# Chunked attention and a feed-forward layer on one core: v's maximum in two halves, an alternating place for weight-block sums, and later hi and lo parts

## Chip, cores and metric

The kernel runs on one core of one Trainium2 chip. The metric is the device time of one execution in microseconds; the median of several runs is compared. Before the change the median of 3 runs is 870.75 us (869.64 to 871.2).

## The reference

Attention inside chunks of 64 positions, then `h = x @ w_in`, `g = h - tanh(h)`, `g @ w_out`, all in float32:

```python
q_c = q.reshape(B, H, nc, chunk, D)          # 8, 8, 9, 64, 64; k and v alike
scores = scale * np.matmul(q_c, k_c.transpose(0, 1, 2, 4, 3))
scores = scores - np.max(scores, axis=-1, keepdims=True)
attn = np.exp(scores)
attn = attn / (np.sum(attn, axis=-1, keepdims=True) + 1e-09)
out = np.matmul(attn, v_c)
...
x = out.transpose(0, 2, 1, 3).reshape(B * S, H * D)     # 4608 x 512
h = x @ w_in                                            # 512 x 2048
g = h - np.tanh(h)
return (g @ w_out).astype(np.float32)                   # 2048 x 512
```

## The kernel before

The 4608 tokens are worked on in nine groups of 512, numbered 0 to 8. Attention fills a group's x; the feed-forward layer then takes the group in units. float32 accuracy is kept by splitting operands into a hi and a lo part (float16 in the later stages) and adding three products.

Groups 0, 1 and 2 go through `FeedForward` (16 units each, one for each block of 128 rows of the hidden layer). Groups 3 to 8 go through `Fast`: 16 units to a group, unit (b, j) taking half the group's tokens (b) and the weight-block pair (j, j + 8). In a unit PE runs `gemm1` (24 matmuls into one of two PSUM tiles `ph`), ACT the tanh (L644), DVE the difference (L645), POOL three sums for a seven-product scheme of the second matrix product (L646 to L648), and one unit later ACT and DVE make hi and lo of it (L657, L658). `gemm2` of a unit follows three units after its `gemm1`; at a new half of the tokens one unit has none and the next has two. `finish` (L688 and its neighbours) turns the PSUM sums of a half into output rows.

While a group is in the feed-forward layer, the next group's attention is prepared between its units. The function `ahead` names the place: `put(unit, part, f)`, where part 0 lies ahead of the unit's gemm2 and part 1 behind it. First comes a common scale: ACT sums |q| and |k| (L107, units 1 and 2), DVE takes the largest |v| (L125, L126, unit 4), PE transposes these `sums` (`across`, L293, unit 4 part 1), DVE takes their maximum over partitions (`most`, L295), and PE spreads it (`spread_out`, L302, unit 5). DVE makes powers of two of it (L119 to L121, L507 to L512). Units 6 and on split q, k and v (L322, L323), multiply scores (L333, unit 8), and so on for the two halves of the group. The raw tensors are loaded two 128-token pairs at a time, in units 7 and 15 of the group before.

The seven-product scheme needs sums of the second weights. For each pair j `Half.combine` adds on POOL: the first sum w1 (L474) into the first free place, then the second (L477) and three more steps (L480 to L485). `Half.shorten` makes hi and lo of the four results on ACT (L502) and DVE (L503). Pairs 0 to 5 are done in group 2's stage; pairs 6 and 7 run over into the first units of `Fast`, placed by a list of positions at the end of the kernel.

Inside these stages the schedule is manual: every engine keeps the order in which the code is written. An engine works its queue strictly in that order, so one instruction that waits holds all behind it.

The step whose place in the queues the prediction speaks of:

```python
largest(some.rearrange("p i n -> p (i n)"), d["sums"][:, 2:3])
```

Of the kernel before, what the change touches and what calls it, by code (L numbers as in the profile page):

```python
# [11 lines left out]
F32 = mybir.dt.float32  # L12
# [6 lines left out]
ALU = mybir.AluOpType  # L19
AX = mybir.AxisListType  # L20
PSUM = bass.MemoryType.PSUM

P = 128
# [16 lines left out]
FAST = 3  # L40
# [19 lines left out]
def attn_ffn_kernel(ctx: ExitStack, tc: tile.TileContext, qE, kE, vE, qL, kL, vL, w_in, w_out, out):  # L60
# [8 lines left out]
    nc = tc.nc  # L69
# [19 lines left out]
    def place_of(a, part, fc, dtype=F16):  # L89

        return w_pool[fc].tile([P, DM], F32R, name=f"w{a}{part}{fc}").bitcast(dtype)
# [8 lines left out]
    def new_half_x():  # L100

        t = xpool.tile([P, KC, MOST], F32R, name="xh").bitcast(F16)
        return t[:, :, :MOST], t[:, :, MOST:]
# [149 lines left out]
    class Late:  # L253
# [14 lines left out]
        def sums(self, g, n, other=None):  # L268
# [13 lines left out]
            if other is None:  # L282
                self.scales(g)

        def scales(self, g):
            self.across(g)
            self.spread_out(g)
# [135 lines left out]
    class Half:  # L423
# [42 lines left out]
        def combine(self, j):  # L466

            (h1, l1), (h2, l2) = ([t.bitcast(F32) for t in wt[fc][1]] for fc in (j, j + FC // 2))  # L470
            names = [(a, 1, fc) for fc in (j, j + FC // 2) for a in "hl"]
            free = self.free
            w1 = place_of(*free[0], F32)
            nc.gpsimd.tensor_add(w1, h1, l1)  # L474
            yield
            w2 = place_of(*names[0], F32)
            nc.gpsimd.tensor_add(w2, h2, l2)  # L477
            yield
            x, y = (place_of(*n, F32) for n in names[1:3])
            nc.gpsimd.tensor_sub(x, w2, w1)  # L480
            yield
            nc.gpsimd.tensor_add(y[:, :HD], w1[:, :HD], w1[:, HD:])
            nc.gpsimd.tensor_add(y[:, HD:], w2[:, :HD], w2[:, HD:])
            yield
            nc.gpsimd.tensor_add(w1[:, HD:], w1[:, :HD], w2[:, HD:])  # L485
            self.sums[j] = w1, x, y, w2[:, HD:]
            parts = [place_of(*n).rearrange("p (a n) -> p a n", a=2) for n in (names[3], free[1], free[2])]
            if j % 2 == 0:
                self.last = place_of(*free[3])
            parts.append(self.last[:, (j % 2) * DM:(j % 2 + 1) * DM].rearrange("p (a n) -> p a n", a=2))  # L490
            self.dest[j] = parts
            self.free = [free[0], *names[:3], *free[3 + (j % 2 == 0):]]
            a, b, c, d = parts
            left, right = slice(0, HD), slice(HD, DM)
            fast_w[j] = {1: a[:, :, right], 2: a[:, :, left], 3: b[:, :, right], 4: b[:, :, left], 5: d, 6: c[:, :, left], 7: c[:, :, right]}
            yield
# [19 lines left out]
    class FeedForward:  # L516
# [54 lines left out]
        def run(self, units, at, ahead=None):  # L571
            for s in range(len(units) + LAG):
                if ahead:
                    ahead(s)
                if s < len(units):
                    self.gemm1(*units[s])
                    self.shrink()
                    self.split()
                for f in at.pop(2 * s, []):
                    f()  # L580
                if len(self.queue) > min(LAG, len(units) + LAG - 1 - s):
                    self.gemm2()
                for f in at.pop(2 * s + 1, []):
                    f()
            assert not at, at
            self.finish()
# [152 lines left out]
    def ahead(att, at, g):  # L739

        o = 2 * FC * (g - FAST)

        def put(unit, part, f, *args):
            at[o + 2 * unit + part].append(lambda: f(*args))

        for unit, n in (1, "q"), (2, "k"), (4, "v"):
            put(unit, 0, lambda n=n: att.sums(g, n, ffn.tile([P, MOST], F32, name="t", bufs=3)))
        put(4, 1, att.across, g)
        put(5, 0, att.spread_out, g)
        put(5, 1, lambda: powers.update({g: half.power_of(g)}))  # L750
        put(6, 0, lambda: xs.update({g: new_half_x()}))
        for b, u in enumerate((6, 14)):
            put(u, 0, att.split, g, b, "q")
            put(u + 1, 0, att.split, g, b, "k")
            put(u + 1, 1, att.split, g, b, "v")
            if g + 1 < NG:
                for i in (2 * b, 2 * b + 1):
                    put(u + 1, 1, att.load, FIRST[g + 1] + i, i)
            put(u + 2, 0, att.scores, g, b)
            put(u + 2, 1, att.shifted, g, b)  # L760
            put(u + 3, 0, att.exponent, g, b)
            put(u + 3, 1, att.totals, g, b)
            put(u + 4, 0, att.divided, g, b)
            put(u + 5, 0, att.transpose, g, b)
            at[o + 2 * u + 16].insert(0, lambda b=b: att.values(g, b, xs[g]))
# [15 lines left out]
    att = Early(pool, [psum, ps_a], 4, warm)  # L781
# [70 lines left out]
    att, half = Late(late), Half(late)  # L852
# [26 lines left out]
    for g in range(FAST, NG):  # L879
        ahead(att, at, g)  # L880
    made = {}

    def make(j, steps):
        if j not in made:
            made[j] = half.combine(j)
        for _ in range(steps):
            next(made[j])
# [5 lines left out]
    o = 2 * FC  # L893
    for k, j, steps in (o - 1, 6, 2), (o + 1, 6, 2), (o + 3, 6, 1), (o + 4, 7, 1), (o + 5, 7, 1), (o + 6, 7, 1), (o + 7, 7, 1), (o + 8, 7, 1):
        at[k].append(lambda j=j, steps=steps: make(j, steps))
    for k, j, some in (o + 6, 6, slice(0, 2)), (o + 8, 6, slice(2, 4)), (o + 11, 7, slice(0, 2)), (o + 15, 7, slice(2, 4)):
        at[k].append(lambda j=j, some=some: half.shorten(j, some))
    at[o + 17].append(lambda: post.extend(place_of(*n, F32) for n in half.free[:3]))
    with tc.manual_schedule():
# [53 lines left out]
```

## Time and profile before

| | us |
|---|---|
| median of 3 runs | 870.75 |
| the profiled execution | 869.55 |
| its span, first to last instruction | 867.8 |
| PE busy | 826.6 |
| DVE busy | 655.5 |
| ACT busy | 469.8 |
| POOL busy | 354.0 |

Rows of instructions read: start, duration, engine, line, operation, output<-inputs, shapes, count, and in brackets the idle time of the engine just ahead with what ended it. A row of the view of waits reads: who waited <- for whom: total us, times, longest. A row of the chain of work that ended last reads: start, duration, what; "issue" is time in which nothing that the profile shows was waited for. A row of a stretch reads: from:to, length, then busy time of PE, PEld (weight loads), DVE, ACT and POOL, the granted clock as a share of full speed, and the DMA share and GB/s. Line numbers are those of the kernel before.

### The profile page before, as it was taken

What the parts mean: (1) busy time and instruction counts of PE and PEld (TensorE: products, weight loads), DVE (VectorE), ACT (ScalarE), POOL (GpSimd) and SP (SyncE); (2) the same over time, 40 slices, a digit from 0 to 9 for tenths busy, and PEclk for the clock granted to TensorE, in tenths of its full rate; (3) what the DMA queues carried; (4) which work ended last, traced back from release to release, by engine and by line L of the source; (5) the groups of instructions that cost most, each with busy time, mean ns of one, the idle gap of its engine ahead of it and who ended that gap; (6) DMA issues with size and microseconds to landing.
All of it is one profiled execution on the core that took longest, in us unless ns stands there. A gap on an engine that the chain in (4) does not pass through costs nothing.

```text
span 867.8 us, 20051 instructions
## 1 busy us (share of the span) xinstructions
PE 826.6 (95%) x8546; PEld 687.9 (79%) x8546; DVE 655.5 (76%) x885; ACT 469.8 (54%) x767; POOL 354.0 (41%) x368
## 2 busy tenths in 40 slices
PE   8999999999999998699979997999799979999996
PEld 6888777788756667588868886888688868888886
DVE  6897896778449988697858786878688777877563
ACT  7698786665345566354725463546444544444332
POOL 0000000000026667555635654565456554756563
PEclk8999999999999999799989999999999999999999
DMA  9973435220202123022212221222122210112000
GB/s 221 260 224 121 147 106 185 74 74 26 74 1 73 26 59 89 2 74 50 75 49 75 51 74 49 75 50 75 50 71 53 75 49 3 39 13 50 2 26 25
DMA packets 61401, 63.16 MB, mean 73 GB/s; under 512 B 32640, under 2 KB 40832, under 8 KB 61312
## 3 DMA queue, kind: packets, MB, share of 16 engines
q1 hardware_dynamic: 61312, 61.88, 25.3%
q8 instruction: 67, 1.10, 0.5%
q14 instruction: 22, 0.18, 0.1%
HBM read 45.09 MB, written 9.44 MB: 63 GB/s over the span
## 4 chain that ended last, share of the span: by engine, by line
PE 83%; DVE 8%; POOL 3%; ACT 3%; issue 3%; DMA 1%; SPq 0%; ACTq 0%; DVEq 0%; POOLq 0%
PE ph L637 27%; PE po L675 22%; PE po L569 14%; PE ph L540 13%; PE psa L333 3%; DVE sums L125 2%; PE psa L243 1%; PE psa L195 1%; DVE wh L688 1%; POOL xl L646 1%; POOL xl L647 1%; DVE gl L658 1%; DVE w L143 1%; ACT wh L657 1%; ACT gh L657 1%
## 5 line engine op out<-in xcount | busy, mean ns | idle before, releaser
L637 PE MATMUL ph<-xh,wl 128*128 128x256 f16 x2160 | 258.8, 279 | 0.0
L637 PEld LDWEIGHTS <-wl 128*128 128x128 f16 x2160 | 215.6, 100 | 29.7 <-issue 0.5
L644 ACT ACTIVATE t<-ph,sig 128x512 f32<-128x512 f32 x96 | 66.0, 687 | 214.7 <-PE ph L637 214.4
L646 POOL TENSOR_TENSOR xl<-xl 128x256 f32<-128x256 f32 x96 | 88.6, 923 | 225.4 <-DVE xl L645 225.4
L645 DVE SCALAR_TENSOR_TENSOR xl<-ph,sig,t 128x512 f32<-128x512 f32 x96 | 71.6, 746 | 82.1 <-ACT t L644 81.6
L675 PEld LDWEIGHTS <-wh 128*128 128x128 f16 x1008 | 97.3, 98 | 11.6
L647 POOL TENSOR_TENSOR xl<-xl 128x128 f32<-128x128 f32 x96 | 104.4, 1087 | 0.0
L675 PE MATMUL po<-wl,wh 128*128 128x256 f16 x576 | 91.7, 273 | 0.0
L648 POOL TENSOR_TENSOR xl<-xl 128x256 f32<-128x256 f32 x96 | 90.1, 939 | 0.0
L658 DVE SCALAR_TENSOR_TENSOR wh<-xl,to_g,wh 128x896 f16<-128x896 f32 x48 | 67.5, 1406 | 25.3 <-ACT wh L657 24.3
L658 DVE SCALAR_TENSOR_TENSOR gl<-xl,to_g,gh 128x896 f16<-128x896 f32 x48 | 75.0, 1563 | 8.4 <-ACT gh L657 8.4
L569 PE MATMUL po<-wh,gh 128*128 128x512 f32 x192 | 78.9, 411 | 0.7 <-ACT gh L559 0.7
L675 PE MATMUL po<-wh,wh 128*128 128x256 f16 x432 | 78.7, 273 | 0.0
L540 PE MATMUL ph<-xh,wl 128*128 128x512 f16 (+2 forms) x324 | 77.0, 375 | 0.0
L569 PE MATMUL po<-wl,gh 128*128 128x512 f32 x192 | 75.5, 393 | 0.0
L569 PE MATMUL po<-wh,gl 128*128 128x512 f32 x192 | 75.2, 396 | 0.0
L657 ACT ACTIVATE wh<-xl,to_g 128x896 f16<-128x896 f32 x48 | 49.7, 1035 | 44.0 <-POOL xl L648 44.0
L675 PEld LDWEIGHTS <-gh 128*128 128x128 f16 x672 | 64.9, 98 | 7.8
L474 POOL TENSOR_TENSOR wh<-wh,wl 128x512 f32<-128x512 f32 x8 | 14.2, 1779 | 107.2 <-DVE wl L463 75.6
L560 DVE TENSOR_TENSOR gl<-t,gh 128x512 fp32r<-128x512 f32 (+1 forms) x52 | 40.7, 785 | 20.3 <-ACT gh L559 18.1
L675 PE MATMUL po<-wh,gh 128*128 128x256 f16 x336 | 54.4, 273 | 0.0
L448 POOL PARTITION_ALL_REDUCE whole<-sums x1 | 0.4, 447 | 130.7 <-DMA rawv<-vL 130.7
(154 smaller groups left out, 1516.9 us busy)
## 6 DMA issues: line engine op xcount, KB each, us to landing
raw<-w_in SPq DMA_DIRECT2D x16, 512.0 KB, 4.0
raw<-w_out SPq DMA_DIRECT2D x16, 512.0 KB, 5.6
out<-wh SPq DMA_DIRECT2D x32, 256.0 KB, 2.2
rawk<-kL SPq DMA_DIRECT2D x28, 256.0 KB, 3.1
rawv<-vL SPq DMA_DIRECT2D x28, 256.0 KB, 3.6
xl<-qL SPq DMA_DIRECT2D x28, 256.0 KB, 3.1
qbd<-qE SPq DMA_DIRECT2D x16, 128.0 KB, 4.3
k<-kE SPq DMA_DIRECT2D x8, 256.0 KB, 4.4
```

What stands on the lines that cost most here:

```text
L540: nc.tensor.matmul(ph, lhsT=self.weight(fc, 0, a)[:, kc * P:(kc + 1) * P], rhs=x[b][:, kc, cols], start=(k == 0), stop=(k == 3 * KC - 1))
L560: nc.vector.tensor_sub(gl, t, gh)
L569: nc.tensor.matmul(self.po[t], lhsT=gg[a][:, ts], rhs=self.weight(fc, 1, b), start=(fc == 0 and i == 0), stop=(fc == FC - 1 and i == 2))
L637: nc.tensor.matmul(self.ph[:, 1 - f::2, :], lhsT=half_w[fc][:, w, kc * P:(kc + 1) * P], rhs=rhs, start=(k == 0), stop=(k == 3 * KC - 1))
L644: nc.scalar.activation(t, self.ph, AF.Tanh, scale=sig)
L645: nc.vector.scalar_tensor_tensor(out=u[:, :4], in0=self.ph, scalar=sig, in1=t, op0=ALU.mult, op1=ALU.subtract)
L646: nc.gpsimd.tensor_add(u[:, 4:6], u[:, 1:3], u[:, 0:4:3])
L647: nc.gpsimd.tensor_add(u[:, 6], u[:, 1], u[:, 2])
L648: nc.gpsimd.tensor_sub(u[:, 0:4:3], u[:, 0:2], u[:, 2:4])
L657: nc.scalar.activation(gh, u, AF.Copy, scale=powers[1])
L658: nc.vector.scalar_tensor_tensor(out=gl, in0=u, scalar=powers[1], in1=gh, op0=ALU.mult, op1=ALU.subtract)
L675: nc.tensor.matmul(place[m], lhsT=part[:, self.SUM[m]], rhs=w[m][:, o], start=first, stop=(j == FC // 2 - 1 and part is gl), skip_group_ch ...
```

## The change

Three edits.

1. A new function `halves` takes the largest |v| over two pairs (1024 elements of each partition) at a time, and joins the two results with the scaling in one small instruction. For groups 4 to 8 the first half stands three units ahead of the group's own first unit (unit 13 of the group before), for group 3 in unit 1; the second half stands in unit 2, part 1. Before, one maximum over 2048 elements stood in unit 4. The scale's other steps keep their places.
2. `combine`: with more than four free places, the first and the last change places before each pair, so that w1 of successive pairs goes to two places in turn.
3. `shorten` of pairs 6 and 7 is placed in later units: (o + 6, 8, 11, 15) becomes (o + 9, 11, 13, 15), counted in half units.

```diff
+        def halves(self, g, i):
+
+            d = self.st[f"g{g}"]
+            if i == 0:
+                d["v"] = self.pool.tile([P, 2], F32, name="v", bufs=2)
+            v = d["v"]
+            nc.vector.tensor_reduce(out=v[:, i:i + 1], in_=self.raw["v"][:, 2 * i:2 * i + 2].rearrange("p i n -> p (i n)"), axis=AX.X, op=ALU.max, apply_absolute_value=True)
+            if i:
+                nc.vector.tensor_scalar(out=d["sums"][:, 2:3], in0=v[:, 0:1], scalar1=v[:, 1:2], scalar2=2.0 ** -12, op0=ALU.max, op1=ALU.mult)
...
             free = self.free
+            if len(free) > 4:
+                free[0], free[-1] = free[-1], free[0]
             w1 = place_of(*free[0], F32)
...
-        for unit, n in (1, "q"), (2, "k"), (4, "v"):
+        for unit, n in (1, "q"), (2, "k"):
             put(unit, 0, lambda n=n: att.sums(g, n, ffn.tile([P, MOST], F32, name="t", bufs=3)))
+        put(-3 if g > FAST else 1, 0, att.halves, g, 0)
+        put(2, 1, att.halves, g, 1)
         put(4, 1, att.across, g)
...
-    for k, j, some in (o + 6, 6, slice(0, 2)), (o + 8, 6, slice(2, 4)), (o + 11, 7, slice(0, 2)), (o + 15, 7, slice(2, 4)):
+    for k, j, some in (o + 9, 6, slice(0, 2)), (o + 11, 6, slice(2, 4)), (o + 13, 7, slice(0, 2)), (o + 15, 7, slice(2, 4)):
         at[k].append(lambda j=j, some=some: half.shorten(j, some))
```

The new lines shift the numbers: L295 becomes L305, L302 becomes L312, L323 L333, L380 L390, L474 L486, L477 L489, L503 L515, L645 L657, L658 L670, L688 L700. L291 is the new maximum, L293 the instruction that joins the halves.

DVE's queue in units 2 to 5 of the period that prepares group 5, before, from the last row of `finish` (L688) on:

```order
L688 SCALAR_TENSOR_TENSOR wh_2610<-po_4610,minus_g,wl_4407 128x256
L645 SCALAR_TENSOR_TENSOR xl<-ph,sig,t 128x512
L658 SCALAR_TENSOR_TENSOR wh_2612<-xl,to_g,wh_2611 128x896
L380 TENSOR_TENSOR a<-s,a 128x2x512
L645 SCALAR_TENSOR_TENSOR xl<-ph,sig,t 128x512
L658 SCALAR_TENSOR_TENSOR wh_2614<-xl,to_g,wh_2613 128x896
L125 TENSOR_REDUCE sums<-rawv 128x1
L126 TENSOR_SCALAR sums<-sums 128x1
L295 TENSOR_REDUCE most<-psa 3x1
```

The same place on DVE now:

```order
L700 SCALAR_TENSOR_TENSOR wh_2610<-po_4612,minus_g,wl_4409 128x256
L291 TENSOR_REDUCE v<-rawv 128x1
L293 TENSOR_SCALAR sums<-v 128x1
L657 SCALAR_TENSOR_TENSOR xl<-ph,sig,t 128x512
L670 SCALAR_TENSOR_TENSOR wh_2612<-xl,to_g,wh_2611 128x896
L390 TENSOR_TENSOR a<-s,a 128x2x512
L657 SCALAR_TENSOR_TENSOR xl<-ph,sig,t 128x512
L670 SCALAR_TENSOR_TENSOR wh_2614<-xl,to_g,wh_2613 128x896
L305 TENSOR_REDUCE most<-psa 3x1
```

The end of the maximum has moved ahead of two units' work; `most` keeps its place behind it. The first half stands on DVE near the end of the period before:

```order
L670 SCALAR_TENSOR_TENSOR wh_2614<-xl,to_g,wh_2613 128x896
L657 SCALAR_TENSOR_TENSOR xl<-ph,sig,t 128x512
L670 SCALAR_TENSOR_TENSOR gl<-xl,to_g,gh 128x896
L291 TENSOR_REDUCE v<-rawv 128x1
L657 SCALAR_TENSOR_TENSOR xl<-ph,sig,t 128x512
```

POOL's queue at the start of `Fast`, before, with the places' own names (wh012 is the free place, wh17 and wl17 are pair 7's weights):

```order
L485 TENSOR_TENSOR wh012_3532<-wh012_3532,wh16_3534 128x256
L646 TENSOR_TENSOR xl_3536<-xl_3536 128x256
L647 TENSOR_TENSOR xl_3536<-xl_3536 128x128
L648 TENSOR_TENSOR xl_3536<-xl_3536 128x2x128
L474 TENSOR_TENSOR wh012_3801<-wh17_100,wl17_101 128x512
```

And now:

```order
L497 TENSOR_TENSOR wh18_3535<-wh18_3535,wh16_3537 128x256
L658 TENSOR_TENSOR xl_3539<-xl_3539 128x256
L659 TENSOR_TENSOR xl_3539<-xl_3539 128x128
L660 TENSOR_TENSOR xl_3539<-xl_3539 128x2x128
L486 TENSOR_TENSOR wh012_3804<-wh17_100,wl17_101 128x512
```

The order on POOL is the same, but pair 6's sum lies in wh18, and pair 7's goes to wh012. DVE's queue in the period that prepares group 4, from `most` to k's split, before (without L119 to L512, which stand behind L658):

```order
L295 TENSOR_REDUCE most<-psa 3x1
L645 SCALAR_TENSOR_TENSOR xl<-ph,sig,t 128x512
L658 SCALAR_TENSOR_TENSOR gl<-xl,to_g,gh 128x896
...
L503 SCALAR_TENSOR_TENSOR wl_3890<-wh_3801,to_w,wl_3890 128x512
L503 SCALAR_TENSOR_TENSOR wh_3891<-wl_3844,to_w,wh_3891 128x512
L645 SCALAR_TENSOR_TENSOR xl<-ph,sig,t 128x512
...
L323 SCALAR_TENSOR_TENSOR a<-rawk,to,a 128x1024
```

And now:

```order
L305 TENSOR_REDUCE most<-psa 3x1
L515 SCALAR_TENSOR_TENSOR wl_3764<-wh_3535,to_w,wl_3764 128x512
L515 SCALAR_TENSOR_TENSOR wh_3765<-wl_3696,to_w,wh_3765 128x512
L657 SCALAR_TENSOR_TENSOR xl<-ph,sig,t 128x512
...
L515 SCALAR_TENSOR_TENSOR wl_3766<-wh_3697,to_w,wl_3766 128x512
L515 SCALAR_TENSOR_TENSOR wh_3767<-wh_3537,to_w,wh_3767 128x256
L657 SCALAR_TENSOR_TENSOR xl<-ph,sig,t 128x512
...
L515 SCALAR_TENSOR_TENSOR wl_3888<-wh_3804,to_w,wl_3888 128x512
L515 SCALAR_TENSOR_TENSOR wh_3889<-wl_3849,to_w,wh_3889 128x512
...
L333 SCALAR_TENSOR_TENSOR a<-rawk,to,a 128x1024
```

Both pairs of pair 6's hi and lo have come in between `most` and k's split; pair 7's first two are still ahead of the split, a unit later than before. PE's and SP's queues read the same before and after, but for line numbers and names.

## The prediction

> **What bounds the kernel now.** I read the page first, then who waited for whom on PE, then PE and DVE in order of time around the longest waits, then the chain that ended last.
>
> ```profile
> span 867.8 us, 20051 instructions
> PE 826.6 (95%) x8546; PEld 687.9 (79%) x8546; DVE 655.5 (76%) x885; ACT 469.8 (54%) x767; POOL 354.0 (41%) x368
> PE psa L293 <- DVE sums L126: 30.0, 6, 9.8
> 443.40:534.17 90.77, 86.07 (x1107) 75.06 (x1107) 69.49 (x83) 44.23 (x54) 49.72 (x52) 0.97 0.23 60
> ```
>
> PE is busy for 95% of the span, and of its 41 us of idle 30.0 are one wait: L293, the transposition that opens a group's scale, for L126, which ends v's maximum. The last row is one period of the Fast stage (length, then PE, PEld, DVE, ACT, POOL busy): DVE works 69.5 of 90.8 us. So DVE is not the bound of a period; it is late at one place of it. PE and DVE there, group 6:
>
> ```profile
> 257.44 0.27 PE L293 MATMUL psa<-ident,sums 128*3 128x128 f32 x1 [1.30 <-DVE sums L126]
> 257.54 2.75 PE L540 MATMUL ph<-xh,wl 128*128 128x512 f16 x12
> 353.85 0.37 PE L293 MATMUL psa<-ident,sums 128*3 128x128 f32 x1 [9.83 <-DVE sums L126]
> 534.17 0.27 PE L293 MATMUL psa<-ident,sums 128*3 128x128 f32 x1 [4.71 <-DVE sums L126]
> 538.66 0.38 PE L302 MATMUL psa<-ident,most 3*128 3x3 f32 x2
> ```
> ```profile
> 524.14 0.48 DVE L688 SCALAR_TENSOR_TENSOR wh<-po,minus_g,wl 128x256 f32<-128x256 f32 x1
> 524.54 0.74 DVE L645 SCALAR_TENSOR_TENSOR xl<-ph,sig,t 128x512 f32<-128x512 f32 x1
> 525.20 1.14 DVE L658 SCALAR_TENSOR_TENSOR wh<-xl,to_g,wh 128x896 f16<-128x896 f32 x1
> ...
> 530.12 1.62 DVE L658 SCALAR_TENSOR_TENSOR wh<-xl,to_g,wh 128x896 f16<-128x896 f32 x1 [1.45 <-ACT wh L657]
> 531.66 2.27 DVE L125 TENSOR_REDUCE sums<-rawv 128x1 f32<-128x2048 f32 x1
> 533.97 0.15 DVE L126 TENSOR_SCALAR sums<-sums 128x1 f32<-128x1 f32 x1
> 534.48 0.28 DVE L295 TENSOR_REDUCE most<-psa 3x1 f32<-3x128 f32 x1 [0.36 <-PE psa L293]
> ```
>
> PE was ready at 534.17 - 4.71 = 529.46. The maximum stood in DVE's queue behind L658 of unit 3, which waited for ACT, which waited for POOL. PE pays twice, since its clock falls while it stands. The 24 matmuls of the next gemm1 in the chain, against an undisturbed one:
>
> ```profile
> 354.22 4.03 PE ph L637 x24
> 360.96 2.62 PE ph L637 x24
> 443.77 5.12 PE ph L637 x24
> ...
> 534.45 4.29 PE ph L637 x24
> ...
> 624.25 3.84 PE ph L637 x24
> ...
> 713.61 5.12 PE ph L637 x24
> ```
>
> **Groups 5 to 8.** Without the 9.83 us of group 4 and the 1.30 us of group 3, the other four waits are 30.0 - 9.83 - 1.30 = 18.9 us. Their slow gemm1s cost 5.12 + 4.29 + 3.84 + 5.12 - 4 x 2.62 = 7.9 us. Together 26.8 us can go.
>
> Not all of it goes. The second half now stands right behind the last L688. No row shows a maximum over 1024 elements into one; the nearest is L365, same input size:
>
> ```profile
> L365 DVE TENSOR_REDUCE sm<-s x14: 1202/1206/1220, 175.7 to 785.4; 128x16 f32<-128x1024 f32 x14
> 529.04 1.04 ACT L657 ACTIVATE wh<-xl,to_g 128x896 f16<-128x896 f32 x1 [3.37 <-POOL xl L648]
> 586.20 0.75 DVE L645 SCALAR_TENSOR_TENSOR xl<-ph,sig,t 128x512 f32<-128x512 f32 x1 [2.41 <-ACT t L644]
> ```
>
> Half costs 1.21 us (bounds 1.14, half of L125's 2.27, and 1.5), and joining the halves 0.15 like L126; with 0.04 between them 1.40 us. The sums are then ready at 524.54 + 1.40 = 525.9, 3.5 us before PE asks, so the wait at L293 is gone. But unit 3's L645 and all that hangs on it (POOL's sums, ACT's L657 at 529.04, DVE's second L658) move back by 1.40. The row L295 (`most`) still stands behind that L658, and L302 on PE needs it. L658 starts at 531.52; its successor began 1.54 us after it (531.66 - 530.12), so `most` runs from 533.06 to 533.34 and L302 can go at 533.4. PE now comes there at 529.46 + 0.27 + 2.62 = 532.35. **A new wait of 1.05 us** takes the place of 4.71 us, four times: 26.8 - 4.2 = **22.6 us**. Behind the waiting L302 stand gemm2 of unit 2 and gemm1 of unit 6, and ACT's next tanh waits for that gemm1; all move with PE and nothing else is late. Bounds: no wait at all (26.8), or POOL's three sums of a unit 1.06 us slower, the spread between this unit and a slow one (18.4).
>
> The first half is in unit 13 of the group before. DVE idles 2.41 us there before L645 at 586.20, waiting for a tanh that waits for PE; 1.21 us fit. Without that cover it would be 1.2 us for each group.
>
> Does the clock fall in a 1.05 us wait? The clock is the last figure but two of this row, for the gemm1 behind the wait of 1.30 us:
>
> ```profile
> 257.50:260.20 2.70, 2.70 (x13) 1.11 (x12) 0.88 (x2) 0.00 (x0) 0.00 (x0) 1.00 0.03 6
> ```
>
> It stayed at 1.00, so I take no. The Trainium skill's page "TensorE: Matmul & The Clock Gate" (Part 1) says the clock halves after one idle window of about 3.4 us, with windows that run free. By it 1.05 us is safe and 4.71 us is not, as the rows show; it also says that a wait between the two may or may not cool PE, which no row here shows and which is a rival below.
>
> **Group 4.** Its 9.83 us have a second cause ahead of the first, in the chain:
>
> ```profile
> 339.51 4.10 issue
> ...
> 343.65 1.72 POOL wh L474
> ...
> 345.43 1.26 POOL wh L477
> 346.69 0.68 POOL xl L646
> ...
> 347.79 0.69 POOL xl L648
> 348.50 1.05 ACT wh L657
> ...
> 351.25 2.28 DVE sums L125
> ```
>
> POOL stands for 4.1 us at L474, the first sum of pair 7, because its place still holds pair 6's, which the hi and lo of pair 6 have not yet read. Unit 3's sums queue behind. With the other place free, L474 starts at 339.55, L477 ends at 339.55 + 1.72 + 0.07 + 1.26 = 342.6, unit 3's sums (346.69 to 348.48) at 344.4, L657 1.07 later at 345.5, DVE's L658 (349.55 to its successor at 351.25) at 347.2, `most` at 347.5. PE comes to L302 at 353.85 - 9.83 + 0.27 + 2.62 = 346.9 and waits 0.6 us. Gain: 9.83 + (4.03 - 2.62) - 0.6 = 10.6 us (9.2 if L474 and L477 run as slowly as any of theirs, 11.2 without a wait).
>
> Part is given back. Two pairs of L503 (pair 6's), which ran while PE stood, now stand behind `most`, and pair 7's first two stay ahead of k's split, which the scores need:
>
> ```profile
> 359.07 0.75 DVE L645 SCALAR_TENSOR_TENSOR xl<-ph,sig,t 128x512 f32<-128x512 f32 x1 [3.56 <-ACT t L644]
> 363.41 0.74 DVE L503 SCALAR_TENSOR_TENSOR wl<-wh,to_w,wl 128x512 f16<-128x512 f32 x1
> 372.70 1.47 DVE L323 SCALAR_TENSOR_TENSOR a<-rawk,to,a 128x1024 f16<-128x1024 f32 x1
> 374.35 0.97 PE L333 MATMUL psa<-a,wh 64*64 64x64 f16 x96
> 376.42 0.47 DVE L503 SCALAR_TENSOR_TENSOR wh<-wh,to_w,wh 128x256 f16<-128x256 f32 x1
> ```
>
> k's split ends at 374.17 and the scores start at 374.35: 0.18 us to spare. The added L503s are 2 x 0.74 and 0.74 + 0.47, less overlap 2.4 us. Some 0.9 us go into the pause before L645 at 359.07 (PE came to L302 at 354.22 + 4.03 = 358.25 there), so 1.3 us are left, and POOL has the rest of pair 7's sums ahead of unit 4's, up to 1 us more. I take 2 us (bounds 0 and 4.5, the second if nothing overlaps and POOL's delay is 2 us). Behind the scores PE has gemm2 of unit 5, which finds its operands ready. Group 4: 10.6 - 2 = **8.6 us**.
>
> **Group 3.** The 1.30 us at 257.44 go: both halves run in pauses of DVE, and the clock had not fallen there. **1.3 us.**
>
> The alternating place also ends POOL's waits at the other L474s. Nothing on PE waited for them, so I count nothing; it costs nothing either, as POOL's work in that stage is the same. The sixth to eighth hi and lo are due only at gemm2 of units 9 and 10.
>
> **The sum.** 22.6 + 8.6 + 1.3 = 32.5 us. The profiled execution took 869.55 us, so 837.1. The median shown is 870.75, 1.2 us more, so 838.3; I forecast **838.0 us**, between the two and nearer to the median.
>
> **The rivals.**
> - *No wait is left at L302 or the scores.* For it: PE, DVE and POOL records of one unit differ by a microsecond. Against: L658 cannot precede POOL's sums. It gives back 4.2 + 0.6 + 2 = 6.8: 831 us.
> - *DVE becomes the pacemaker.* For it: 69.5 us of work in a period that shrinks to about 85, and k's split is 0.18 us ahead of the scores already. Against: at L302 every queue stands as far ahead of PE as before or further. If half of the 22.6 comes back, 849 us.
> - *The moved hi and lo eat group 4.* The scores there wait for all 8.6 us: 846 to 847 us.
> - *The new waits cool PE too.* Each of five then loses what the cheapest cold gemm1 lost, 3.84 - 2.62 = 1.2, or the dearest, 2.5: 844 to 850 us. The 257.44 row speaks against it; the page on the clock gate, as told above, against it too unless a wait passes its window.
> - *Slower.* The halves are read earlier, and a late load of raw v would hold all of DVE at L291. Rows of the load and of its time to land:
>
> ```profile
> 599.92 0.43 SPq L266 DMA_DIRECT2D rawv<-vL  x1
> rawv<-vL SPq DMA_DIRECT2D x28, 256.0 KB, 3.6
> ```
>
> The second half's data land at 603.5; its reader comes a period (some 90 us) after 524.5, near 614. So 10 us are spare. Only a landing 10 + 32.5 / 5 = 17 us later in each of five groups makes the kernel slower.
>
> **How the numbers follow.** Forecast with its bounds 0.65; no waits 0.13; DVE as pacemaker 0.09; hi and lo 0.06; cold clock 0.04; slower 0.03. The range takes in the first three but for the far end of the third: best 831; worst, with the bounds of groups 5 to 8 (4.2) and of group 4 (1.4 + 2.5), 838 + 8.1 = 846. So 831 to 846. About 0.2% is what a measurement of this kernel can tell from no change. All cases but the last are over 2% faster; of the last 0.01 is same and 0.02 slower: 0.97, 0.01, 0.02.
>
> **What would show it.** PE should show no wait at the transposition of `sums` (the old L293), and a wait of about 1 us for `most` at the old L302 in groups 5 to 8, with gemm1 after the transposition at 2.62 us. In group 4 POOL should start pair 7's first sum near 339.5, and PE wait some 2 us at the scores near 364 (347.5 plus the 374.35 - 358.25 = 16.1 us that lie between them now). It is wrong if gemm1 stays at 4 us or more, if the wait for `most` is over 2 us, or if waits appear at PE's gemm1 for free PSUM.

## The result and the profile after

The changed kernel takes 839.65 us (median of 4 runs, 838.4 to 841.22), the kernel before 870.25 us (4 runs, 869.64 to 871.2). The ratio is 0.9648, with a 95% interval of 0.9629 to 0.9668. 838.0 us was forecast, so 1.65 us were missing; the range of 831 to 846 us holds the time. The profiled execution took 839.77 us, where 837.1 was worked out for it.

The page of the changed kernel, its span and busy times:

```profile
span 837.6 us, 20052 instructions
PE 817.3 (98%) x8544; PEld 685.0 (82%) x8546; DVE 657.1 (78%) x891; ACT 470.1 (56%) x767; POOL 357.5 (43%) x368
```

The span is 30.2 us shorter. DVE's and POOL's work has grown by 1.6 and 3.5 us, and PE's busy time has fallen by 9.3 us for the same matmuls. Most of that is the clock: by the rows of the prediction the slow gemm1s had cost 7.9 us in groups 5 to 8 and 1.41 in group 4, and some 1.5 us are lost anew in group 4, as shown below. All that PE still waits for in the stages of the change (from 235 us on), in the view of waits:

```profile
PE psa L312 <- DVE most L305: 6.1, 5, 1.5
PE psa L343 <- DVE a L333: 1.9, 1, 1.9
PE psa L343 <- DVE from L119: 0.7, 1, 0.7
```

The 30.0 us of waits at the transposition (now L303) are gone. New are five waits for `most` at L312, once in each group from 4 on, and two waits in group 4: for the scale's values (L119) and for k's split (L333). Group 6 on PE and DVE in order of time, the same place as was shown of before:

```profile
515.76 0.27 PE L303 MATMUL psa<-ident,sums 128*3 128x128 f32 x1
515.87 2.78 PE L649 MATMUL ph<-xh,wl 128*128 128x256 f16 x24
519.82 0.38 PE L312 MATMUL psa<-ident,most 3*128 3x3 f32 x2 [1.17 <-DVE most L305]
```
```profile
510.60 0.48 DVE L700 SCALAR_TENSOR_TENSOR wh<-po,minus_g,wl 128x256 f32<-128x256 f32 x1
511.00 1.21 DVE L291 TENSOR_REDUCE v<-rawv 128x1 f32<-128x1024 f32 x1
512.24 0.21 DVE L293 TENSOR_SCALAR sums<-v 128x1 f32<-128x1 f32 x1
...
517.95 1.62 DVE L670 SCALAR_TENSOR_TENSOR wh<-xl,to_g,wh 128x896 f16<-128x896 f32 x1 [1.44 <-ACT wh L669]
519.50 0.27 DVE L305 TENSOR_REDUCE most<-psa 3x1 f32<-3x128 f32 x1
```

The sums are ready at 512.45 and PE asks for them at 515.76, 3.3 us later. `most` still stands behind L670, and PE stands 1.17 us for it. The rows of stretches show what the clock does (its figure is the last but two): one whole period, the stretch of the wait, and the stretch behind it:

```profile
431.36:515.76 84.40, 83.24 (x1109) 73.88 (x1107) 69.56 (x85) 44.23 (x54) 49.74 (x53) 1.00 0.26 64
516.00:519.80 3.80, 2.65 (x25) 2.13 (x22) 2.36 (x4) 2.09 (x3) 2.63 (x5) 1.00 0.73 137
519.82:522.40 2.58, 2.58 (x23) 2.33 (x24) 2.51 (x6) 0.55 (x1) 1.89 (x2) 1.00 0.00 0
```

A period takes 84.4 us where it took 90.8, DVE's work in it is the same 69.6 us, and the clock stays at 1.00 over the wait. Group 4 reads otherwise. Its three waits on PE:

```profile
346.61 0.38 PE L312 MATMUL psa<-ident,most 3*128 3x3 f32 x2 [1.50 <-DVE most L305]
...
352.75 0.97 PE L343 MATMUL psa<-s,wh 64*64 64x64 f16 x96 [0.75 <-DVE from L119]
...
365.68 1.32 PE L343 MATMUL psa<-a,wh 64*64 64x64 f16 x92 [1.87 <-DVE a L333]
```

And the rows of stretches before and behind the last of them:

```profile
362.00:364.00 2.00, 1.81 (x20) 1.37 (x18) 2.00 (x4) 2.00 (x3) 1.01 (x1) 1.00 0.46 123
...
365.68:370.38 4.70, 4.70 (x113) 3.85 (x113) 4.70 (x6) 1.35 (x2) 3.01 (x3) 0.64 0.66 195
```

Behind a wait of 1.87 us the clock falls, to 0.64 as the mean of the next 4.70 us (92 of the 96 matmuls of the scores and one gemm2). No term of the prediction has this.

Where the 30.2 us come from can be read from when PE's L302 (now L312) starts in each group:

| L312 of group | before | after | gained since the row above |
|---|---|---|---|
| 3 | 260.23 | 258.62 | 1.61 |
| 4 | 358.18 | 346.61 | 9.96 |
| 5 | 448.82 | 435.41 | 1.84 |
| 6 | 538.66 | 519.82 | 5.43 |
| 7 | 628.02 | 604.22 | 4.96 |
| 8 | 718.66 | 688.62 | 6.24 |
| the span's end | 867.8 | 837.6 | 0.16 |

Group 5 alone should have gained its old wait of 4.71 and its slow gemm1's 2.50 less the new wait of 1.16, that is 6.05 us. The row has 1.84. The missing 4.21 us are what group 4 gives back between its own L312 and the next: 0.75 and 1.87 us of waits, and the clock.

### The profile page after: what moved, and what is told of

Its sections match the earlier page's. It is cut to its first block, busy times and chain, and to the rows that moved or that the text cites. A ratio compares the mean times of both kernels' runs of the same rounds, so it can differ in the third digit from the quotient of the medians.

```text
span 837.6 us, 20052 instructions
## 1 busy us (share of the span) xinstructions
PE 817.3 (98%) x8544; PEld 685.0 (82%) x8546; DVE 657.1 (78%) x891; ACT 470.1 (56%) x767; POOL 357.5 (43%) x368
## 4 chain that ended last, share of the span: by engine, by line
PE 80%; DVE 10%; POOL 4%; ACT 3%; issue 2%; DMA 1%; SPq 0%; ACTq 0%; DVEq 0%
PE ph L649 24%; PE po L687 22%; PE po L581 14%; PE ph L552 14%; PE psa L343 3%; DVE gl L670 1%; POOL xl L658 1%; PE psa L243 1%; DVE wh L670 1%; DMA raw<-w_out 1%; POOL xl L659 1%; PE psa L195 1%; DVE w L143 1%; DVE wh L700 1%; ACT gh L669 1%
## 5 line engine op out<-in xcount | busy, mean ns | idle before, releaser
L649 PE MATMUL ph<-xh,wl 128*128 128x256 f16 x2160 | 249.4, 273 | 0.0
L649 PEld LDWEIGHTS <-wl 128*128 128x128 f16 x2160 | 211.2, 98 | 25.0 <-issue 0.5
L658 POOL TENSOR_TENSOR xl<-xl 128x256 f32<-128x256 f32 x96 | 93.5, 974 | 206.7 <-DVE xl L657 206.7
L657 DVE SCALAR_TENSOR_TENSOR xl<-ph,sig,t 128x512 f32<-128x512 f32 x96 | 71.6, 745 | 60.2 <-ACT t L656 60.1
L660 POOL TENSOR_TENSOR xl<-xl 128x256 f32<-128x256 f32 x96 | 90.0, 938 | 0.0
L670 DVE SCALAR_TENSOR_TENSOR wh<-xl,to_g,wh 128x896 f16<-128x896 f32 x48 | 67.5, 1406 | 20.8 <-ACT wh L669 19.8
L670 DVE SCALAR_TENSOR_TENSOR gl<-xl,to_g,gh 128x896 f16<-128x896 f32 x48 | 73.2, 1525 | 9.6 <-ACT gh L669 9.4
L687 PE MATMUL po<-wl,gh 128*128 128x256 f16 x336 | 53.1, 275 | 0.0
L572 DVE TENSOR_TENSOR gl<-t,gh 128x512 fp32r<-128x512 f32 (+1 forms) x52 | 38.6, 744 | 17.8 <-ACT gh L571 15.6
```

The source lines that it names most:

```text
L572: nc.vector.tensor_sub(gl, t, gh)
L649: nc.tensor.matmul(self.ph[:, 1 - f::2, :], lhsT=half_w[fc][:, w, kc * P:(kc + 1) * P], rhs=rhs, start=(k == 0), stop=(k == 3 * KC - 1))
L657: nc.vector.scalar_tensor_tensor(out=u[:, :4], in0=self.ph, scalar=sig, in1=t, op0=ALU.mult, op1=ALU.subtract)
L658: nc.gpsimd.tensor_add(u[:, 4:6], u[:, 1:3], u[:, 0:4:3])
L660: nc.gpsimd.tensor_sub(u[:, 0:4:3], u[:, 0:2], u[:, 2:4])
L670: nc.vector.scalar_tensor_tensor(out=gl, in0=u, scalar=powers[1], in1=gh, op0=ALU.mult, op1=ALU.subtract)
```

## The experiments

Each kernel was timed in rounds with the kernel before on the same chip (870.11, 869.92 and 869.98 us there).

**The halves alone.** From the changed kernel, the alternating place and the later hi and lo are taken out:

```diff
-            if len(free) > 4:
-                free[0], free[-1] = free[-1], free[0]
...
-    for k, j, some in (o + 9, 6, slice(0, 2)), (o + 11, 6, slice(2, 4)), (o + 13, 7, slice(0, 2)), (o + 15, 7, slice(2, 4)):
+    for k, j, some in (o + 6, 6, slice(0, 2)), (o + 8, 6, slice(2, 4)), (o + 11, 7, slice(0, 2)), (o + 15, 7, slice(2, 4)):
```

> The halves alone; the alternating place and the later hi and lo are taken back. Theory (the place matters in group 4 alone): groups 3 and 5 to 8 as in the changed kernel (wait of 1.2 us for `most` at the old L302 in each of 5 to 8). In group 4 POOL's first sum of pair 7 waits for hi and lo of pair 6 again, near 344, and PE waits 8 to 10 us, now at the old L302 and no longer at L293, with a cold clock after it: 839.65 + 6.6 = 846 us (844 to 848). Rival (the halves alone do it, the place only tidies POOL): 839 to 841 us.

Measured: 843.52 us (842.86 to 844.58), ratio 0.9691 (0.9677 to 0.9705). That is just faster than the theory's 844 to 848 and slower than the rival's 841. The halves alone bring 26.6 us; groups 5 to 8 and group 3 are as in the changed kernel, and group 4 waits 7.08 us at L312, where 8 to 10 were forecast. POOL's and DVE's rows say why:

```profile
342.93 1.71 POOL L484 TENSOR_TENSOR wh<-wh,wl 128x512 f32<-128x512 f32 x1 [4.38 <-DVE wl L513]
344.72 1.26 POOL L487 TENSOR_TENSOR wh<-wh,wl 128x512 f32<-128x512 f32 x1
345.94 0.72 POOL L656 TENSOR_TENSOR xl<-xl 128x256 f32<-128x256 f32 x1
346.62 0.45 POOL L657 TENSOR_TENSOR xl<-xl 128x128 f32<-128x128 f32 x1
347.03 0.72 POOL L658 TENSOR_TENSOR xl<-xl 128x256 f32<-128x256 f32 x1
```
```profile
339.91 1.14 DVE L668 SCALAR_TENSOR_TENSOR wh<-xl,to_g,wh 128x896 f16<-128x896 f32 x1
340.97 1.22 DVE L390 TENSOR_TENSOR a<-s,a 128x1024 f16<-128x1024 f32 x1
...
343.43 0.74 DVE L655 SCALAR_TENSOR_TENSOR xl<-ph,sig,t 128x512 f32<-128x512 f32 x1
348.87 1.75 DVE L668 SCALAR_TENSOR_TENSOR wh<-xl,to_g,wh 128x896 f16<-128x896 f32 x1 [4.69 <-ACT wh L667]
```

(The lines of this kernel are two lower than those of the changed one.) POOL stands 4.38 us at pair 7's first sum until pair 6's hi and lo have been read, as the prediction had it for the kernel before. The rows carry a second thing that matters below: unit 3's three sums take 345.94 to 347.75, 1.81 us, while DVE does nothing. Behind the wait the clock is cold, 0.56 over the next 4.79 us:

```profile
352.86:357.65 4.79, 4.79 (x25) 3.63 (x26) 3.37 (x11) 2.27 (x3) 4.05 (x6) 0.56 0.00 0
```

**The other two edits without the halves.** v's maximum is one piece in unit 4 again:

```diff
-        for unit, n in (1, "q"), (2, "k"):
+        for unit, n in (1, "q"), (2, "k"), (4, "v"):
...
-        put(-3 if g > FAST else 1, 0, att.halves, g, 0)
-        put(2, 1, att.halves, g, 1)
```

> The alternating place and the later hi and lo without the halves: one maximum over 2048 in unit 4 as before. Theory: groups 5 to 8 wait 4.7 us at L293 again with a cold clock, group 3 waits 1.3; in group 4 the wait falls from 9.8 to 3.5 to 4.5 us, and 2 us come back at the scores: 866 us (863 to 868). Rival (the place is what moved all periods): below 855. Rival (the place does nothing without the halves): 870.

Measured: 868.67 us (866.6 to 869.01, 7 runs), ratio 0.9975 (0.9964 to 0.9986), less than the least gain that was expected, but a gain beyond its uncertainty. The waits at the transposition stay: 1.30 us in group 3, 4.70 in groups 5 to 8, and 7.07 in group 4 instead of 9.83:

```profile
PE psa L303 <- DVE sums L126: 27.2, 6, 7.1
PE psa L343 <- DVE a L333: 0.7, 1, 0.7
```

So these two edits bring 1.4 us by themselves and 3.0 to 3.9 us beside the halves. Group 4's wait falls by 2.76 us here, and beside the halves the place alone also takes 2.76 us off it (7.08 to 4.32, below). But here the scores wait 0.69 us, and PE goes from the transposition to L312 in 5.42 us at a clock of 0.50, where before it took 4.33 at 0.64. The forecast of 3.5 to 4.5 us for group 4's wait was missed by 2.6 us or more. A part of that is that the two sums of pair 7 and unit 3's three take 6.2 us on POOL here, beside DVE's work (339.89 to 346.08), and took 4.8 before (343.65 to 348.46).

**One maximum, moved, not halved.** All 2048 elements in unit 2, part 1, with the other two edits:

```diff
-        put(-3 if g > FAST else 1, 0, att.halves, g, 0)
-        put(2, 1, att.halves, g, 1)
+        put(2, 1, lambda: largest(att.raw["v"][:, :SIZES[g]].rearrange("p i n -> p (i n)"), att.st[f"g{g}"]["sums"][:, 2:3]))
```

> The maximum is moved to unit 2 part 1 but not halved (2048 elements at once, for all groups from 3 on); the rest as in the changed kernel. Theory (most of the gain is the place, and the halving is worth what it takes off DVE ahead of unit 3): the waits for `most` grow from 1.17 to 2.2 us in groups 5 to 8 and by 1.1 in group 4, no wait at L293: 839.65 + 5.4 = 845 us (843 to 846.5). Rival (only the place counts): 839 to 841. Rival (only the halving counts): 860 or more.

Measured: 844.54 us (842.55 to 846.79), ratio 0.9694 (0.9678 to 0.971). PE waits 2.16 us at L312 in groups 5 to 8 where it waits 1.16 with halves. PE in groups 6 and 8, and the stretch behind group 6's wait:

```profile
523.43 0.38 PE L312 MATMUL psa<-ident,most 3*128 3x3 f32 x2 [2.16 <-DVE most L305]
...
694.25 0.38 PE L312 MATMUL psa<-ident,most 3*128 3x3 f32 x2 [2.16 <-DVE most L305]
...
697.78 3.53 PE L649 MATMUL ph<-xh,wl 128*128 128x256 f16 x24
```
```profile
523.43:526.00 2.57, 2.57 (x23) 2.33 (x24) 2.50 (x6) 0.00 (x0) 1.89 (x2) 1.00 0.01 1
```

Most of the gain is the move: 868.67 - 844.54 = 24.1 us against the same two edits without it. The halving is worth 4 to 5 us more. Behind three of the four waits of 2.16 us the clock stayed at 1.00. Behind group 8's it fell, to 0.70 as the mean of 5.75 us: the next gemm1 starts 3.53 us after L312 (2.61 in group 6) and takes 3.53 us (2.78 in group 6), 1.7 us lost in all in the traced execution (846.79 us, the slowest of the four).

**The hi and lo at their old places**, with the halves and the alternating place:

```diff
-    for k, j, some in (o + 9, 6, slice(0, 2)), (o + 11, 6, slice(2, 4)), (o + 13, 7, slice(0, 2)), (o + 15, 7, slice(2, 4)):
+    for k, j, some in (o + 6, 6, slice(0, 2)), (o + 8, 6, slice(2, 4)), (o + 11, 7, slice(0, 2)), (o + 15, 7, slice(2, 4)):
```

> Halves and alternating place; hi and lo of pairs 6 and 7 in their old units. Theory: the two small hi-lo steps of unit 4 stand ahead of `most` again, so group 4's wait for it grows from 1.5 to about 3 us, and the waits at group 3's values (0.75) and group 4's scores (1.9), 2.65 us together, go: 838.5 us (837 to 840). Rival (the later units are what makes group 4 fast): 842 us or more.

Measured: 840.17 us (840.13 to 841.41), ratio 0.9655 (0.964 to 0.9669). It lies just above the theory's end and short of the rival, and the time, the same as the changed kernel's, comes about in another way: no wait at the values or the scores, but 4.32 us for `most` in group 4, and a cold clock behind it. Some 3 us were forecast for that wait. The two steps ahead of `most` alone take 1.99 us here (348.84 to 350.83), beside work of POOL, where the rows of the prediction have 0.74 and 0.47.

```profile
PE psa L312 <- DVE most L305: 9.0, 5, 4.3
```
```profile
352.00:355.00 3.00, 3.00 (x16) 2.13 (x15) 1.28 (x2) 2.27 (x3) 3.00 (x4) 0.50 0.00 0
```

The third edit beside the other two is thus worth nothing that can be measured: it trades 2.8 us of wait at L312, and its clock, for the waits at the values and the scores, and theirs.

**The changed kernel again**, in the next batch:

> The changed kernel once more, beside the next two on the same chip: 839.65 us (838.5 to 841).

Measured: 840.54 us (839.86 to 841.06), ratio 0.9661 (0.9648 to 0.9674), with the same waits (1.52 and 1.16 us at L312, 0.75 at the values, 1.88 at the scores). The clock behind the scores' wait falls here too, to 0.86, 0.50 and 0.78 in the three slices of 2 us from 366 us on. The numbers of group 4 are no accident of one execution.

**The maximum's end and the transposition a unit earlier.**

```diff
-        put(2, 1, att.halves, g, 1)
-        put(4, 1, att.across, g)
+        put(1, 1, att.halves, g, 1)
+        put(3, 1, att.across, g)
```

> The changed kernel with the second half of the maximum in unit 1 part 1 and the transposition with `most` (across) in unit 3 part 1, so that `most` stands ahead of the second L670 on DVE. Theory (the wait left at the old L302 is `most` behind unit 3's L670, and nothing else is late there): the waits of 1.17 us in groups 5 to 8 go (4.7 us); group 4 trades its 1.5 us for some 1 us at the transposition, as the sum of |k| ends late there, and gains 0 to 1: 834.5 us (833 to 836.5). Rival (PE is held by DVE's load, and the wait moves to the next meeting point, scores or PSUM): 838 to 840.

Measured: 835.77 us (834.39 to 836.23), ratio 0.9604 (0.9591 to 0.9617). `most` now stands ahead of the L670 that holds it, and none of the five waits at L312 is left. Group 4 keeps three others:

```profile
PE psa L343 <- DVE from L119: 2.4, 1, 2.4
PE psa L343 <- DVE a L333: 1.9, 1, 1.9
PE psa L303 <- ACT t L107: 1.0, 1, 1.0
```
```profile
367.00:370.00 3.00, 1.15 (x95) 1.09 (x95) 3.00 (x3) 2.16 (x4) 3.00 (x3) 1.00 0.13 14
```

The waits at L312 were thus the price of `most` standing behind L670, as the prediction had it. The second fence shows the stretch of the scores: the wait is as long as the changed kernel's, and the clock stays at 1.00. So the time is within the theory's range by some luck. Not in the theory was that the wait for the values grows from 0.75 to 2.44 us; what made up for most of it is the clock, 1.5 us (worked out below), which the theory did not have either.

**The same, with the hi and lo at their old places:**

> The same with hi and lo of pairs 6 and 7 in their old units. Theory: with `most` ahead of them they cannot delay it, and less is left ahead of group 4's scores: the same as the kernel with the later units or up to 2 us faster, 833.5 us (832 to 836). Rival (in group 4 DVE and POOL are the bound, whatever the order): within 0.5 us of the kernel with the later units.

Measured: 834.89 us (834.7 to 835.66), ratio 0.9598 (0.9585 to 0.9612). With `most` early, the old places are at least as good: the scores' wait falls to 0.81 us, while that for the values is 3.07 us, and the transposition's 1.04 stays. The 0.88 us between this kernel and the one with the later units are less than the spread of that one's runs (834.39 to 836.23), so theory and rival are not told apart.

**Pair 7's first hi and lo behind k's split**, all else as in the changed kernel:

```diff
-(o + 13, 7, slice(0, 2))
+(o + 15, 7, slice(0, 2))
```

> The changed kernel with one thing moved: the first hi and lo of pair 7 go from unit 6, part 1 to unit 7, part 1, so that in group 4 they stand behind k's splitting on VectorE and not ahead of it. Theory one (group 4 gives back 1.9 us because TensorE's scores wait for that splitting, and some 1.5 us more because the gemms after the wait run at a granted clock of 0.5 to 0.7): the scores wait of 1.87 us goes, the slices after 366 us show 1.00, and the time is 836 to 838 us. The two instructions take 0.75 us each ahead of the split, so a wait of up to 0.4 us may stay. Rival one (the clock falls there for another reason, and only the wait goes): 838 to 839 us. Rival two (the wait moves on to the next thing in VectorE's queue, the scores' maximum or v's splitting): 839.5 to 841 us, as the changed kernel.

Measured: 837.14 us (836.86 to 838.05), ratio 0.9624 (0.961 to 0.9637), as theory one has it. The waits, and the row of the same work as the changed kernel's stretch from 365.68 to 370.38:

```profile
PE psa L312 <- DVE most L305: 6.1, 5, 1.5
PE psa L343 <- DVE from L119: 0.7, 1, 0.7
PE psa L343 <- DVE a L333: 0.5, 1, 0.5
```
```profile
364.39:367.56 3.17, 3.17 (x113) 2.89 (x113) 3.17 (x4) 2.68 (x5) 1.93 (x2) 1.00 0.52 123
```

The same 113 matmuls take 3.17 us at a clock of 1.00 and took 4.70 at 0.64: 1.53 us for the clock. The wait is shorter by 1.32. Together 2.85 us; the spans differ by 837.6 - 834.8 = 2.8, the medians by 2.5 (and by 3.4 from the run again).

**The same move in the kernel with the early maximum and the old hi and lo places:**

> The kernel of e7 (v's second half in unit 1, the maximum over the partitions in unit 3, hi and lo of pair 6 at the places of before) with the first hi and lo of pair 7 in unit 7, part 1. Theory one: of e7's two waits in group 4 the scores' 0.81 us goes; the values' 3.07 us stays, since it is made by VectorE's wait of 2.13 us for ScalarE's gelu halves and not by hi and lo: 833.5 to 834.5 us. Rival: hi and lo ahead of it in unit 5 made the values late too; then the values' wait falls to about 1.5 us and the time is 832 to 833 us. If nothing moves but the two instructions: 834.9 us as e7.

Measured: 834.84 us (834.39 to 835.15), ratio 0.9594 (0.9581 to 0.9607), no different from 834.89. The scores' wait is gone and the values' stays at 3.07 us, as theory one says, but the 0.8 us are not seen in the time, which is just above that theory's end. In the profiled execution (835.15 us, the longest of the five) the clock took them. The row of the stretch behind the values' wait, first in the kernel with the early maximum and all hi and lo at their old places, then here:

```profile
356.00:359.70 3.70, 3.70 (x40) 3.31 (x36) 3.56 (x10) 1.51 (x2) 0.77 (x1) 1.00 0.02 4
```
```profile
356.00:359.70 3.70, 3.70 (x21) 2.67 (x20) 2.93 (x8) 1.99 (x4) 2.29 (x3) 0.54 0.02 4
```

In the same time PE gets through 40 matmuls in the one and 21 in the other, after waits of the same 3.07 us. Of the other four executions only the mean granted clock is on record, 0.998 against 0.992 in this one. That speaks for their not having cooled there, but the mean also holds the start (in the first 20 us the clock was 0.83 in this trace, and 1.00 in that of the early maximum with later hi and lo), so it is not shown. If they did not cool, why they were no faster stays open. Both kernels beat the changed one by about 5 us, and they are the fastest that were run.

One combination wasn't tried: later hi and lo with a single place for the sums. Not run, but read from the order of POOL's queue: pair 7's first sum would there wait for hi and lo that in turn wait for sums behind it.

## Why the prediction was right, point by point

- **Groups 5 to 8, 22.6 us: right.** Measured are 6.05 + 5.43 + 4.96 + 6.24 = 22.7 us (6.05 as worked out for group 5, the others as read). The sums are ready 3.3 us before PE asks (3.5 forecast), the gemm1 behind takes 2.62 us, and the new wait is 1.16 us (1.05 forecast). It comes from the place of `most` behind L670: with `most` ahead of it (the early maximum) it is gone, and with a maximum a microsecond longer (the one that was moved whole) it is a microsecond longer. The first half in unit 13 costs nothing: the pause of 2.41 us before the next L657 became one of 1.28. DVE there:

```profile
564.87 1.21 DVE L291 TENSOR_REDUCE v<-rawv 128x1 f32<-128x1024 f32 x1
567.36 0.75 DVE L657 SCALAR_TENSOR_TENSOR xl<-ph,sig,t 128x512 f32<-128x512 f32 x1 [1.28 <-ACT t L656]
```

- **Group 3, 1.3 us: right.** L312 comes 1.61 us earlier. Group 2's was already 0.15 us earlier (158.63 against 158.78), so some 1.46 us are group 3's.
- **Group 4 up to L312, 10.6 us: nearly.** 9.96 us were gained. POOL no longer stands at pair 7's first sum, but PE waits 1.50 us there, not 0.6. The step that was off is the time of unit 3's three sums, taken over as 1.8 us from the kernel before, where DVE stood still beside them. Now they run beside DVE's work, in POOL's and DVE's order of time:

```profile
337.87 1.27 POOL L486 TENSOR_TENSOR wh<-wh,wl 128x512 f32<-128x512 f32 x1
339.22 1.27 POOL L489 TENSOR_TENSOR wh<-wh,wl 128x512 f32<-128x512 f32 x1
340.45 1.57 POOL L658 TENSOR_TENSOR xl<-xl 128x256 f32<-128x256 f32 x1
341.98 1.44 POOL L659 TENSOR_TENSOR xl<-xl 128x128 f32<-128x128 f32 x1
343.38 0.73 POOL L660 TENSOR_TENSOR xl<-xl 128x256 f32<-128x256 f32 x1
```
```profile
339.28 2.16 DVE L670 SCALAR_TENSOR_TENSOR wh<-xl,to_g,wh 128x896 f16<-128x896 f32 x1
341.36 1.74 DVE L390 TENSOR_TENSOR a<-s,a 128x1024 f16<-128x1024 f32 x1
```

They take 3.66 us (340.45 to 344.11), twice the 1.81 of the first experiment, and DVE's two take 2.16 and 1.74 us where they took 1.14 and 1.22 there, while POOL stood. L486 and L489 made up some 0.5 us of it, with 2.58 us (337.87 to 340.45) instead of 3.05, and unit 3's L670 some 0.6, with 1.07 us to its successor instead of 1.70. The rows of the kernel before held the warning: over its 96 units the three sums take 0.92, 1.09 and 0.94 us on average, 2.95 together.

- **Group 4 behind L312, 2 us given back: the term that was mis-sized.** It measured 4.2 us. The mechanism that was named, pair 7's hi and lo ahead of k's split, makes the scores wait 1.87 us near 364, as forecast ("some 2 us"); the next to last experiment removes it by moving those two instructions. Not in the term were the clock behind that wait, 1.53 us, shown by the same experiment, and the wait of 0.75 us for the values at 352.75. L119 stands in DVE's queue behind an L670 that waits for ACT, and that for POOL, which still had pair 7's sums to do; the prediction had put this delay of POOL at the scores. The three make 4.15 of the 4.21 us. The bound given for the give-back, 4.5 us, held, but for other reasons than those that made it.
- **The rivals.** No wait left (831 us) is refuted by the rows, DVE as pacemaker too: every period shrank to 84.4 us, with the same work of DVE. The moved hi and lo did not eat group 4: the scores wait 1.87 us, not 8.6. That the new waits cool PE is refuted for the five waits at L312, and came true for one that the rival did not name, the scores' in group 4. No late load of v: L291 follows the row ahead of it without a pause.

So the forecast of 32.5 us is 2.3 over the 30.2 of the spans: 2.2 too much for the rest of group 4 and 0.6 for the way to its L312, less 0.3 up to group 3's L312 (0.15 of it ahead of group 3), 0.1 in groups 5 to 8 and 0.2 at the end that it had too little.

## What to carry to other kernels

When a late instruction is moved forward, ask at once which instruction of the same scale or sum still stands at the old place: it sets the next wait, as `most` did here, and moving it too gained 4 to 5 us more. Take the time of an instruction that moves from a row in which its neighbours on the other engines work as they will at the new place, not from a row in which one of them stood still. And price a wait on PE with the clock that may fall behind it: 1.9 us of wait were 3.4 us of time in the changed kernel, and no more than themselves in the one with the early maximum.

## What was not expected of the hardware

**The clock falls after shorter waits than the longest that leave it alone.** Behind all 24 waits of 1.15 to 1.52 us at L312 (in the changed kernel, its second run and four variants) it stayed at 1.00. Behind the four waits of 2.16 us in one execution it stayed at 1.00 three times and fell to 0.70 once. Of four waits of 1.86 to 1.88 us at the scores, the one in the kernel with the early maximum left it at 1.00, and the three others (the changed kernel, its second run, the maximum that was moved whole) were followed by a lower clock, 0.64 in the first. Of two waits of 3.07 us one left it at 1.00 and one was followed by 0.54. After 4.32 and 7.08 us it was 0.50 and 0.56. So between about 1.9 and 3.1 us the length of the wait alone doesn't decide.

The page "TensorE: Matmul & The Clock Gate" of the Trainium skill (Part 1) has the clock halve after an idle window of about 3.4 us, with windows that run free of the kernel. What the prediction has it say of waits between 1.05 and 4.71 us is worked out from these two statements and no sentence of it. That the place of the wait in a window decides would fit the four waits of 2.16 us, which stand at the same place of the program. But a wait of 1.87 or 2.16 us is no whole window of that length, so if the windows are as the Trainium skill has them, one that is idle in part was enough here. Around the scores' wait PE also runs small matmuls (64x64, four of them ahead of it and 92 behind); whether that matters is not shown. No run here moved a wait against the windows, so this is left open.

**POOL and DVE slow each other.** The same three sums took 1.81 us with DVE still and 3.66 us beside L670 and L390. The Trainium skill's page "SBUF — State Buffer" (Who interferes with whom) says that a DVE instruction with two inputs in SBUF contends with a GpSimd instruction that reads SBUF, and both of these are of that kind. The trace agrees, and gives the price that mattered here: about 0.85 us for a sum of 128x256 (0.72 to 1.57), 1.0 for one of 128x128 (0.45 to 1.44), and 1.0 for DVE's 128x896 (1.14 to 2.16). DVE's L657, which reads one of its inputs from PSUM, is not slowed: its 96 rows in the changed kernel have a mean of 0.745 us, and POOL's third sum, which ran beside it, took 0.73.
